# A fold product split in two, and the front's order written anew, in a fused linear attention and feed-forward kernel

## The chip, the cores and the metric

One core of one Trainium2 chip runs the kernel. TensorE (PE in the profile) does matrix products; VectorE (DVE), ScalarE (ACT) and GpSimd (POOL) work beside it, and SyncE (SP) issues transfers. The metric is the device time of one execution in microseconds.

## The reference

Linear attention with the map phi(x) = elu(x) + 1, over 8 batches of 8 heads with 576 positions of 64 numbers; its output, as 4608 rows of 512, goes through a multiplicative feed-forward.

```python
def phi(x):
    return np.where(x > 0, x, np.exp(x) - 1.0) + 1.0
q_p, k_p = (phi(q), phi(k))
kv = np.einsum('bhsd,bhse->bhde', k_p, v)
z = np.sum(k_p, axis=2)
num = np.einsum('bhsd,bhde->bhse', q_p, kv)
den = np.einsum('bhsd,bhd->bhs', q_p, z)[..., None] + 1e-06
...
a = x @ w1
b = x @ w2
h = a * b @ w3
return (h @ w_out).astype(np.float32)
```

x is num / den with the heads side by side. w1 and w2 are 512 x 1024, w3 is 1024 x 1024, w_out is 1024 x 512; all arrays are float32.

## The kernel before

The kernel multiplies w3 by w_out first (the fold) and keeps the result, wf, in bf16; so a row needs x w1, x w2, their product and one product with wf. The 4608 rows are 36 tiles of 128, and four tiles are a chunk: chunks 0 to 8. There is no scheduler: the string ORDER lists some 780 short steps, and each engine runs its share of them in that order. Waits between engines are derived from the tiles that steps read and write; a tile whose pool has no free buffer waits for the release of an older one. So a step's place fixes three things: what it stands behind on its engine, which buffer its tile gets, and whose release it waits for.

The steps that matter here (x is a batch or chunk, and so on):

- le0 to le7 (line 191) load eighths of w3, lo0 to lo3 (181) quarters of w_out, each 128 x 1024, with a cast to bf16, from POOL's queue. lw (171) loads blocks of w1 and w2. lk, lq, lv (165) load k, q, v of a batch, whole or as halves, from POOL with a + at the end and else from SP. POOL's transfers share eight semaphores in turn, so the ninth waits until the first has landed.
- H (152) are matmuls on zeros that keep TensorE running. wt (202) transposes an eighth of w3, wc (206) copies it out of PSUM, wm i.k0.k1 (212) multiplies the pieces k0 to k1 of eighth i with w_out; eight pieces are one product of the fold, and lo0 holds pieces 0 and 1, lo1 2 and 3, lo2 4 and 5, lo3 6 and 7. wd (216) copies the product to wf.
- xk, xq (226, exp on ScalarE), yk, yq (230) and zk, zq (237, both VectorE) make phi of half a batch.
- Batches 0 and 1 take another way than the rest: Z (349) sums k, K (261) makes kv, qa (330) transposes q on TensorE and qb (336) copies it, kz (361) copies kv and z, e (372) makes numerators and denominators, er (387, 388) and em (392) divide; rm (405) and rd (412, 413 on ScalarE, 415 on VectorE) do the same for the rest rows. From batch 2 on T (274) and D (320) transpose by DMA from SP, A (286) makes the product and G (304 to 308) divides.
- g c.f.w.h (428) is a first product of chunk c: w is 0 for w1 and 1 for w2; h is 0 or 1 for a half of two matmuls, 2 for all four. fc (439) copies the w1 side out, fm (448, or 446 in chunk 8) multiplies the two. O (456) is the product with wf, eight matmuls; oc (460) copies it into an o_sb tile, on VectorE with a + and else on ScalarE; S (468) stores it with two DMAs; Q8.3 (479 to 481) is the last tile.

Pools that matter: mm_ps has four banks of PSUM for wf, a, b and o products; at_ps has two buffers of two banks for the attention; o_sb has six buffers, which the a_sb of five f of chunk 0 share (line 436). A PSUM bank is freed by the copy that reads it.

At the top of ORDER all eight eighths of the fold are done as two steps of four matmuls, for example wm1.0.4 and wm1.4.8. Stores go from POOL, and for chunk 8 from SP (line 467).

Of the kernel before, what the change touches and what calls it, by code (L numbers as in the profile page):

```python
# [34 lines left out]
g1.6.1.0 rd1 g1.0.0.0 fm1.4 lq3.2 g1.3.1.1 g1.0.0.1 xk2.0 fm1.3 lv3.2 g1.6.1.1 g1.6.0.0 zk2.1 fc1.0 g1.6.0.1
g1.0.1.0 zk2.0 fc1.6 lk4.2 g1.5.0.0 fm1.6 K2.0 K2.1 g1.0.1.1 kc2.1 kc2.0+ g1.5.1.0 fm1.0 A2.0 A2.1 g1.2.1.0
G2.0 g1.2.0.0 g1.5.0.1 g1.5.1.1 fc1.5 g1.2.1.1 g1.2.0.1 fm1.5 D2.0 A2.3 fc1.2 A2.2 O0.2 yq3.1 xq3.1 fm1.2
xk3.0 G2.1 O0.1 O1.1 oc0.1 yk3.0 D2.1 xk3.1 zq3.1 O1.2 lq4.2 xk4.1 oc1.1+ zk3.0 xq3.0 A2.4 yq3.0 g2.4.0.2
yk3.1 lv5.2 g2.5.0.2 fc2.4 zq3.0 g2.5.1.2 fc2.5 G2.2 T3.1 oc1.2 g2.7.0.2 oc0.2 yk4.1 g2.4.1.2 fc2.7 vc3.0+
T3.0 g2.7.1.2 xq4.0 fm2.5 g2.2.0.2 vc3.1 zk3.1 g2.1.1.2 fm2.7 fc2.2 lv4.2 K3.0 K3.1 g2.1.0.2 kc3.1+ lk5.2  # L40
fm2.4 g2.0.0.2 fc2.1 S0.2 kc3.0 fm2.1 g2.3.0.2 xq4.1 yk4.0 g2.6.0.2 S1.1 zk4.1 fc2.0 g2.2.1.2 fc2.6 yq4.0
A3.0 xk4.0 g2.6.1.2 fm2.2 A3.1 O1.0 G3.0 g2.3.1.2 oc1.0 zk4.0 fc2.3 g2.0.1.2 S1.0 fm2.6 A3.3 A3.2 S0.0 O1.3
fm2.3 fm2.0 S0.1 G3.1 O2.2 oc1.3 D3.0 O2.1 oc2.2 vc5.0+ D3.1 vc4.1 yq4.1 lq5.2 O2.0 oc2.1 zq4.0 S2.2 vc4.0
# [2 lines left out]
g3.1.1.2 xq5.0 zq5.1 D2.2 g3.5.1.2 fm3.1 S1.2 K4.0 K4.1 fm3.5 fc3.2 g3.0.1.2 kc4.0 kc4.1+ fc3.3 zq5.0 A4.1
A4.0 g3.2.1.2 G4.0 T5.0 g3.0.0.2 g3.3.1.2 fm3.2 K5.0 D4.0 K5.1 fm3.3 fc3.0 g3.6.1.2 S1.3 kc5.0 fm3.0 A4.2
g3.7.1.2 kc5.1+ S2.1 A4.3 fm3.7 g3.6.0.2 T5.1 G4.1 fc3.6 g4.2.0.2 g4.2.1.2 fc4.2 lv6.2 g4.5.0.2 fm4.2 lq6.2
g4.3.0.2 fm3.6 fc4.5 g4.0.0.2 fc4.3 lk6.2 O3.1 fc4.0 A5.0 oc3.1+ O3.0 A5.1 oc3.0 g4.1.0.2 G5.0 S3.1 g4.5.1.2
vc6.0 D4.1 g4.0.1.2 fm4.5 g4.3.1.2 fm4.0 fc4.1 D5.0 g4.6.0.2 xq6.1 fm4.3 A4.4 g4.6.1.2 G4.2 fc4.6 g4.7.1.2  # L50
xq6.0 yq6.0 O3.3 lq7.2 yq6.1 xk6.0 fm4.6 g4.1.1.2 lk7.2 xk6.1 oc3.3+ A5.4 O3.2 fm4.1 S3.3 G5.2 D4.2 g4.7.0.2
oc3.2 zq6.0 g5.7.0.2 vc6.1+ fc4.7 g5.4.0.2 yk6.1 fc5.7 A5.2 D5.2 fm4.7 fc5.4 g4.4.0.2 zq6.1 g4.4.1.2 fc4.4
zk6.1 T6.1 xq7.0 g5.3.0.2 fm4.4 g5.3.1.2 xq7.1 yq7.0 O4.2 T6.0 yq7.1 fc5.3 zq7.0 xk7.1 O4.3 fm5.3 S3.2 oc4.2
yk7.1 xk7.0 S4.2 zq7.1 g5.7.1.2 zk7.1 oc4.3 g5.2.0.2 S4.3 fm5.7 g5.2.1.2 fc5.2 yk7.0 g5.6.0.2 S3.0 fm5.2
# [21 lines left out]
def kernel(  # L76
# [385 lines left out]
    def o_store(c, m):  # L462
        kind, b, t = order[c * (NCH // P) + m]
        for g in range(2):
            bb, j = (b, 2 * t + g) if kind == "J" else (b + g, NJ - 1)
# [2 lines left out]
            queue.dma_start(out=out[bb * S:(bb + 1) * S, :].rearrange("(p j) n -> p j n", j=NJ)[:, j, :],  # L468
                            in_=o_sbs[c, m][part])

# [128 lines left out]
```

## Time and profile before

| what | us |
|---|---|
| three runs | 246.41, 244.14, 246.7; median 246.41 |
| the profiled execution's own time | 244.84 |
| its span, first to last instruction | 243.1 |
| TensorE busy | 232.2 |
| VectorE, ScalarE, GpSimd busy | 148.9, 118.4, 60.2 |
| first fold matmul starts | 13.76 |
| first matmul of a first product starts | 33.49 |
| last matmul ends, by the chain of waits | 239.31 |

Times inside the profile count from the span's start. A row of the timeline has a start, a length, the engine (SPq for SyncE's queue), the line, the operation, what it writes and reads, how many instructions are merged, and in brackets the idle time ahead of it on that engine with what ended it. A row of a tile's view has shortest, median and longest duration in ns and the first and the last start; the line on landing gives the time from issue to landing for the instructions in that view.

### The profile page before, as it was taken

The numbers are of one execution on the slowest core, as the hardware profiler recorded it, in microseconds if no ns is written. First come the engines' busy times: TensorE is split into PE (matmuls) and PEld (weight loads), VectorE is DVE, ScalarE is ACT, GpSimd is POOL, SyncE is SP. The second block draws the span as 40 slices with busy tenths as digits, with TensorE's granted clock in tenths as the row PEclk, the third lists the DMA queues.
The fourth block names the chain that finished last, engine by engine and source line by source line (L and its number), as shares of the span: only waits on it lengthen the run. The fifth ranks groups of instructions, "written<-read, shape, count | busy, mean of one in ns | idle before, by whom it ended". The sixth has DMA issues, their size and how long they took to land.

```text
span 243.1 us, 4808 instructions
## 1 busy us (share of the span) xinstructions
PE 232.2 (96%) x1938; PEld 112.1 (46%) x1955; DVE 148.9 (61%) x280; ACT 118.4 (49%) x177; POOL 60.2 (25%) x104
## 2 busy tenths in 40 slices
...
PEclk9999999999999999999999999999999999999999
DMA  6999999998899999998699999795540002321125
GB/s 151 194 283 325 213 255 296 294 387 299 186 395 200 370 263 332 205 272 275 105 256 381 216 373 152 293 122 151 155 119 1 0 3 86 97 86 46 43 79 137
DMA packets 48470, 49.20 MB, mean 202 GB/s; under 512 B 30528, under 2 KB 34880, under 8 KB 48448
## 3 DMA queue, kind: packets, MB, share of 16 engines
...
q14 instruction: 7, 0.06, 0.1%
...
## 4 chain that ended last, share of the span: by engine, by line
PE 89%; DMA 4%; DVE 2%; ACT 1%; POOL 1%; issue 1%; POOLq 0%
PE b_ps L428 25%; PE o_ps L456 25%; PE a_ps L428 24%; PE wf_ps L212 6%; DMA wo<-in_moe_w_out_dram 4%; PE nd L286 3%; PE kvp L261 2%; POOL w3b L191 1%; PE w3p L202 1%; PE o_ps L479 1%; PE nd L372 1%; PE tq L330 1%; PE zp L349 1%; DVE k L237 1%; DVE ab L448 1%
## 5 line engine op out<-in xcount | busy, mean ns | idle before, releaser
L428 PEld LDWEIGHTS <-w_sb 128*128 128x128 bf16 x576 | 54.9, 98 | 63.9 <-issue 1.4
L468 POOL DMA_DIRECT2D out_dram<-o_sb x64 | 36.3, 571 | 157.1 <-ACT o_sb L460 72.8
L428 PE MATMUL b_ps<-xt,w_sb 128*128 128x512 bf16 x288 | 70.7, 379 | 0.0
L428 PE MATMUL a_ps<-xt,w_sb 128*128 128x512 bf16 x288 | 69.5, 379 | 0.4 <-DVE xt L392 0.3
L439 ACT COPY a_sb<-a_ps 128x512 f32<-128x512 f32 x72 | 41.7, 585 | 57.6 <-PE a_ps L428 41.6
L456 PE MATMUL o_ps<-wf_sb,ab 128*128 128x512 bf16 x266 | 63.2, 379 | 0.8 <-issue 0.2
L448 DVE TENSOR_TENSOR ab<-a_sb,b_ps 128x512 bf16<-128x512 f32 x64 | 45.8, 730 | 27.7 <-PE b_ps L428 17.8
L456 PEld LDWEIGHTS <-ab 128*128 128x128 bf16 x280 | 26.7, 98 | 31.0 <-issue 0.5
L460 ACT COPY o_sb<-o_ps 128x512 f32<-128x512 f32 x23 | 13.3, 585 | 38.4 <-PE o_ps L456 31.5
L226 ACT ACTIVATE e<-k 128x1152 bf16<-128x1152 f32 x16 | 18.3, 1161 | 12.3 <-DMA k<-in_k_dram 12.3
L226 ACT ACTIVATE e<-q 128x1152 bf16<-128x1152 f32 x16 | 18.4, 1163 | 2.4 <-DMA q<-in_q_dram 2.4
L212 PE MATMUL wf_ps<-wo,w3t 128*128 128x512 bf16 x61 | 14.7, 379 | 1.6 <-DMA wo<-in_moe_w_out_dram 1.3
L230 DVE TENSOR_SCALAR r<-k 128x1152 bf16<-128x1152 f32 x16 | 11.9, 749 | 6.1 <-DMA k<-in_k_dram 6.1
L308 DVE TENSOR_TENSOR xn<-nd,r 128x512 bf16<-128x512 f32 x24 | 15.4, 683 | 0.0
L230 DVE TENSOR_SCALAR r<-q 128x1152 bf16<-128x1152 f32 x16 | 12.5, 804 | 3.3 <-DMA q<-in_q_dram 3.3
L446 DVE TENSOR_TENSOR ab<-a_sb,b_ps 128x512 bf16<-128x512 f32 x8 | 5.5, 686 | 14.1 <-PE b_ps L428 9.4
L460 DVE COPY o_sb<-o_ps 128x512 f32<-128x512 f32 x12 | 8.3, 690 | 9.3 <-PE o_ps L456 9.0
L237 DVE TENSOR_TENSOR k<-e,r 128x1152 bf16<-128x1152 bf16 x16 | 11.8, 752 | 0.6 <-ACT e L226 0.5
L237 DVE TENSOR_TENSOR q<-e,r 128x1152 bf16<-128x1152 bf16 x16 | 11.8, 749 | 0.3
L286 PEld LDWEIGHTS <-qt 128*128 128x128 bf16 (+1 forms) x120 | 8.6, 100 | 7.2 <-issue 2.7
L286 PE MATMUL nd<-kvb,qt 128*128 128x130 bf16 (+1 forms) x120 | 11.2, 222 | 0.0
L212 PEld LDWEIGHTS <-w3t 128*128 128x128 bf16 x64 | 5.8, 98 | 8.2 <-DVE w3t L206 1.3
...
## 6 DMA issues: line engine op xcount, KB each, us to landing
...
q<-in_q_dram POOLq DMA_DIRECT2D x3, 576.0 KB, 10.4
...
```

The lines of the kernel that those rows point to most:

```text
L212: nc.tensor.matmul(wfs[i], w3ts[i][:, kc, :], wos[0][:, kc, :], start=(kc == 0), stop=(kc == FC - 1))
L226: nc.scalar.activation(out=es[name, b, c], in_=raw[name, b][:, 2 * c:2 * c + 2, :], func=AF.Exp)
L230: nc.vector.tensor_scalar(out=rs[name, b, c], in0=raw[name, b][:, 2 * c:2 * c + 2, :], scalar1=0.0, scalar2=1.0, op0=ALU.max, op1=ALU.add)
L237: nc.vector.tensor_tensor(out=ph[name, b][:, c].rearrange("p j a d -> p a j d"), in0=es[name, b, c].rearrange("p a (j d) -> p a j d", j=NJ ...
L286: nc.tensor.matmul(nd[0:n, u, 2 * c * (D + 1):2 * (c + 1) * (D + 1)], w, kvb[b % 2][:, u, c].rearrange("p a e -> p (a e)"), start=True, st ...
L308: nc.vector.tensor_tensor(out=dst.rearrange("p (i u) e -> p u i e", u=2), in0=v4[:, :, :, 0:D], in1=r[0:n].unsqueeze(3).to_broadcast([n, 2 ...
L428: nc.tensor.matmul(fps[c, f, w], (w1_sb, w2_sb)[w][:, kc, f * P:(f + 1) * P], xt[:, 4 * c:4 * c + 4, kc, :], start=(first and n == 0), sto ...
L439: nc.scalar.copy(out=fsb[c, f], in_=fps[c, f, 0])
L448: nc.vector.tensor_tensor(out=abs_[c][:, f].rearrange("p (m t g) -> p m g t", g=2, t=R), in0=fsb[c, f].rearrange("p (m g t) -> p m g t", g ...
L456: nc.tensor.matmul(o_pss[c, m], abs_[c][:, f, m * P:(m + 1) * P], wf_sb[:, f, :], start=(f == 0), stop=(f == FC - 1))
L460: copy_of(alt)(out=o_sbs[c, m], in_=o_pss[c, m])
L468: queue.dma_start(out=out[bb * S:(bb + 1) * S, :].rearrange("(p j) n -> p j n", j=NJ)[:, j, :], in_=o_sbs[c, m][part])
```

## The change

The first half of each fold product, four matmuls, becomes two steps of two: wm1.0.4 is now wm1.0.2 and wm1.2.4, so its first two matmuls need only lo0. The steps up to chunk 1 stand in a new order; from g2.4.0.2 on TensorE's order is as before. The warm-up is 11 + 3 + 2 + 3 matmuls instead of 12 + 3. Some copies change between VectorE and ScalarE. Loads come in another order: lo0 third instead of sixth, both halves of v0 ahead of k1, q2 ahead of v1. On SP, T2.0 and T2.1 stand ahead of the loads of q3 and k3. On POOL the store S0.3 moves from ahead of S0.2 to between S4.2 and S4.3; the other stores keep their order. Stores of chunk 7 go from SP instead of POOL. ORDER is one line longer, so line numbers behind it are larger by one.

The diff, cut to the lines that the text speaks of:

```diff
-i2 lq0.0 H12 le3 le0 i0 le4 le1 lo1 xq0.0 yq0.0 lo0 lo2 wt3 lo3 H3 lk0.0+ wt0 le6 wc0+ lk0.1+ wc3+ wt4 zq0.0
-le2 wt1 wc4+ lq0.1+ wc1+ qa0.0 le5 wm1.0.4 wm3.0.4 lk1.1+ wm4.0.4 le7 wm3.4.8 wm4.4.8 xk0.0 yk0.0 wm0.0.4
...
-fc0.5 g0.6.0.0 lq2.2+ g0.6.0.1 fc0.1 yk1.0 g0.1.1.0 fc0.6 g0.1.1.1 lv2.2+ g0.4.0.1 xk1.0 fm0.1 g0.2.0.0
-g0.2.0.1 fc0.4 g0.7.0.0 zk1.0 lk2.2+ g0.7.0.1 xq1.0 zk1.1 g0.0.1.0 g0.3.0.0 yq1.0 g0.3.0.1 fc0.7 g0.0.1.1
-zq1.0 xq1.1 Z1.0 Z1.1 fm0.0 qa1.0 fc0.3 g0.3.1.0 qb1.0+ kz1.1.1 g0.2.1.0 kz1.1.0 g0.3.1.1 yq1.1 fc0.2 e1.0.1
...
-em1.0.0 er1.1.0 e1.1.0 oc0.3+ O0.0 em1.1.1 S0.3 xq2.0 em1.1.0 g1.1.0.0 xq2.1 lk3.2 yq2.1 g1.7.0.0 g1.4.0.0
...
-zq4.1 A3.4 yk5.0 O2.3 T4.1 xk5.1 yk5.1 xk5.0 G3.2 g3.7.0.2 oc2.0 g3.1.0.2 zk5.1 D3.2 fc3.7 g3.4.1.2 oc2.3+
-T4.0 fc3.1 zk5.0 g3.4.0.2 vc5.1+ g3.3.0.2 fc3.4 S2.0 xq5.1 fm3.4 g3.5.0.2 yq5.1 g3.2.0.2 S2.3 fc3.5 yq5.0
...
+i2 lq0.0 H11 le6 le0 lo0 i0 le3 le1 lo1 xq0.0 yq0.0 i1 le4 wt6 lo2 H3 wc6+ lo3 zq0.0 wt0 lk0.1+ H2 wc0 i3
+wm6.0.2 lk0.0+ wm0.0.2 qa0.0 le2 wt3 H3 wc3+ lq0.1+ wm3.0.2 wt1 le5 wm3.2.4 wc1+ wm6.2.4 qb0.0+ wm1.0.2
+lv0.1+ wm1.2.4 wm0.2.4 wt4 lv0.0+ le7 wm0.4.8 wm1.4.8 wc4+ wd0 yk0.1 wm6.4.8 xk0.1 wm4.0.2 yk0.0 xk0.0
+wm3.4.8 zk0.1 wm4.2.4 wd3 lk1.0+ wt2 zk0.0 wd1 lw0.2 wc2+ Z0.0 xq0.1 lw0.0 Z0.1 kz0.1.0+ wm4.4.8 lk1.1+
...
+em0.0.0 e0.1.0 er0.1.0 wm7.0.2 em0.1.1 wm7.2.4 em0.0.1 lw1.2 wm7.4.8 wd2 em0.1.0 g0.5.0.0 wd7 g0.7.0.0
+lq2.2+ yk1.0 xk1.0 g0.5.0.1 rm0 g0.7.0.1 lv1.0+ fc0.5 zk1.0 g0.0.0.0 g0.0.0.1 fc0.7 wd5+ g0.1.0.0 lv1.1+
+fc0.0 g0.3.0.0 yk1.1 xk1.1 g0.3.0.1 g0.1.0.1 lk2.2+ g0.4.0.0 fc0.3 zk1.1 g0.2.0.0 Z1.0 fc0.1 lv2.2+ Z1.1
+kz1.1.0+ xq1.0 g0.2.0.1 yq1.0 g0.3.1.0 g0.3.1.1 rd0 zq1.0 g0.4.0.1 g0.2.1.0 fm0.3 fc0.2 qa1.0 fc0.4 g0.6.0.0
...
+yk5.0 O2.3 T4.1 xk5.1 yk5.1 xk5.0 G3.2 g3.7.0.2 oc2.0 g3.1.0.2 zk5.1 D3.2 fc3.7 S2.0 g3.4.1.2 oc2.3+ T4.0
...
+fm5.3 lv7.2 oc4.2 yk7.1 xk7.0 S4.2 zq7.1 g5.7.1.2 zk7.1 oc4.3 S0.3 g5.2.0.2 fm5.7 g5.2.1.2 fc5.2 S4.3 yk7.0
...
-            queue = nc.sync if c == NT * P // NCH - 1 else nc.gpsimd
+            queue = nc.sync if c >= NT * P // NCH - 2 else nc.gpsimd
```

More of the change, by code (lines that the diff above doesn't have):

```diff
@@ L19 @@
 ORDER = """
-i2 lq0.0 H12 le3 le0 i0 le4 le1 lo1 xq0.0 yq0.0 lo0 lo2 wt3 lo3 H3 lk0.0+ wt0 le6 wc0+ lk0.1+ wc3+ wt4 zq0.0
-le2 wt1 wc4+ lq0.1+ wc1+ qa0.0 le5 wm1.0.4 wm3.0.4 lk1.1+ wm4.0.4 le7 wm3.4.8 wm4.4.8 xk0.0 yk0.0 wm0.0.4
-wm1.4.8 qb0.0 zk0.0 wt6 i1 wd1 wm0.4.8 wc6+ xk0.1 yk0.1 wm6.0.4 wd3 lv0.0+ zk0.1 wt2 Z0.0 wd0 lv0.1+ wd4+
-Z0.1 wc2 wm6.4.8 lw0.2 kz0.1.0+ kz0.1.1+ xq0.1 lw0.0 wm2.0.4 yq0.1 i3 e0.0.1 wt5 zq0.1 er0.0.1 lw1.0 wm2.4.8
-wc5+ lk1.0+ er0.0.0 yk1.1 wm5.0.4 lw0.1 wt7 lq1.0+ xk1.1 qa0.1 wc7+ lq1.1+ wm5.4.8 qb0.1+ wd2 K0.0 lw1.1 wd6
@@ L35 @@
[L35 to L43, printed above, removed]
-zq4.1 A3.4 yk5.0 O2.3 T4.1 xk5.1 yk5.1 xk5.0 G3.2 g3.7.0.2 oc2.0 g3.1.0.2 zk5.1 D3.2 fc3.7 g3.4.1.2 oc2.3+
@@ L45 @@
-T4.0 fc3.1 zk5.0 g3.4.0.2 vc5.1+ g3.3.0.2 fc3.4 S2.0 xq5.1 fm3.4 g3.5.0.2 yq5.1 g3.2.0.2 S2.3 fc3.5 yq5.0
[L46 to L54, printed above, removed]
@@ new lines @@
+lv0.1+ wm1.2.4 wm0.2.4 wt4 lv0.0+ le7 wm0.4.8 wm1.4.8 wc4+ wd0 yk0.1 wm6.4.8 xk0.1 wm4.0.2 yk0.0 xk0.0
+wm3.4.8 zk0.1 wm4.2.4 wd3 lk1.0+ wt2 zk0.0 wd1 lw0.2 wc2+ Z0.0 xq0.1 lw0.0 Z0.1 kz0.1.0+ wm4.4.8 lk1.1+
+yq0.1 wm2.0.2 lw0.1 kz0.1.1+ e0.0.1 zq0.1 wm2.2.4 er0.0.0 wt5 lw1.1 wm2.4.8 wc5+ er0.0.1 wd6+ wm5.0.2 lq1.0+
+qa0.1 wd4 K0.0 qb0.1+ lw1.0 K0.1 wm5.2.4 kz0.0.1 wt7 kz0.0.0 e0.1.1 wc7+ e0.0.0 lq1.1+ er0.1.1 wm5.4.8
+em0.0.0 e0.1.0 er0.1.0 wm7.0.2 em0.1.1 wm7.2.4 em0.0.1 lw1.2 wm7.4.8 wd2 em0.1.0 g0.5.0.0 wd7 g0.7.0.0
@@ new lines @@
+lq2.2+ yk1.0 xk1.0 g0.5.0.1 rm0 g0.7.0.1 lv1.0+ fc0.5 zk1.0 g0.0.0.0 g0.0.0.1 fc0.7 wd5+ g0.1.0.0 lv1.1+
+fc0.0 g0.3.0.0 yk1.1 xk1.1 g0.3.0.1 g0.1.0.1 lk2.2+ g0.4.0.0 fc0.3 zk1.1 g0.2.0.0 Z1.0 fc0.1 lv2.2+ Z1.1
+kz1.1.0+ xq1.0 g0.2.0.1 yq1.0 g0.3.1.0 g0.3.1.1 rd0 zq1.0 g0.4.0.1 g0.2.1.0 fm0.3 fc0.2 qa1.0 fc0.4 g0.6.0.0
+qb1.0+ g0.1.1.0 xq1.1 g0.1.1.1 yq1.1 e1.0.1 g0.2.1.1 kz1.1.1 zq1.1 er1.0.1 g0.6.0.1 fm0.1 g0.5.1.0 g0.5.1.1
+fm0.2 er1.0.0 g0.4.1.0 g0.4.1.1 fm0.5 qa1.1 fc0.6 g0.7.1.0 fm0.4 g0.7.1.1 qb1.1 yq2.1 g0.6.1.0 g0.0.1.0
@@ new lines @@
+fm0.7 xq2.1 g0.6.1.1 g0.0.1.1 fm0.6 e1.1.1 xq2.0 K1.0 fm0.0 zq2.1 K1.1 er1.1.0 O0.3 yq2.0 kz1.0.0 zq2.0
+kz1.0.1 e1.0.0 er1.1.1 T2.0 e1.1.0 em1.0.1 O0.0 em1.0.0 oc0.3 em1.1.0 xk2.0 T2.1 g1.1.0.0 em1.1.1 g1.1.1.0
+g1.4.0.0 oc0.0 yk2.1 g1.4.0.1 xk2.1 g1.1.0.1 lq3.2 g1.1.1.1 g1.7.0.0 lk3.2 fc1.1 zk2.1 g1.7.0.1 g1.6.0.0
+fm1.1 fc1.7 g1.6.0.1 fc1.4 yk2.0 g1.3.1.0 lv3.2 g1.6.1.0 fc1.6 vc2.1+ g1.4.1.0 g1.6.1.1 vc2.0+ g1.3.1.1
+g1.4.1.1 zk2.0 g1.3.0.0 g1.3.0.1 fm1.6 rm1 K2.0 fm1.4 K2.1 g1.2.0.0 kc2.1 kc2.0+ lk4.2 g1.2.0.1 fc1.3
@@ new lines @@
+g1.7.1.0 rd1 fm1.3 g1.7.1.1 g1.5.1.0 fm1.7 fc1.2 g1.0.1.0 A2.1 A2.0 g1.2.1.0 G2.0 g1.0.0.0 g1.2.1.1 g1.0.0.1
+g1.0.1.1 fc1.0 g1.5.1.1 fm1.2 D2.0 A2.2 A2.3 g1.5.0.0 G2.1 g1.5.0.1 O0.2 fc1.5 xq3.1 fm1.5 D2.1 O0.1 xq3.0
+fm1.0 lq4.2 yq3.1 xk3.1 O1.1 zq3.1 xk3.0 yk3.0 A2.4 O1.2 oc1.1+ zk3.0 yq3.0 g2.4.0.2 oc1.2 yk3.1 lv5.2 oc0.1
+g2.5.0.2 fc2.4 zq3.0 g2.5.1.2 fc2.5 G2.2 T3.1 g2.7.0.2 oc0.2 S0.2 g2.4.1.2 yk4.1 fc2.7 xq4.0 g2.7.1.2 vc3.0+
+T3.0 S1.1 fm2.5 g2.2.0.2 vc3.1 zk3.1 g2.1.1.2 lv4.2 fc2.2 fm2.7 K3.0 xk4.1 K3.1 g2.1.0.2 kc3.1+ fm2.4 lk5.2
@@ new lines @@
+g2.0.0.2 fc2.1 kc3.0 fm2.1 g2.3.0.2 xq4.1 yk4.0 g2.6.0.2 zk4.1 fc2.0 g2.2.1.2 fc2.6 yq4.0 A3.0 xk4.0
+g2.6.1.2 fm2.2 A3.1 O1.0 G3.0 g2.3.1.2 oc1.0 zk4.0 D3.0 fc2.3 g2.0.1.2 S1.0 fm2.6 A3.3 A3.2 S0.0 O1.3 fm2.3
+fm2.0 S0.1 G3.1 O2.2 oc1.3 O2.1 oc2.2 vc5.0+ D3.1 vc4.1 S2.2 yq4.1 lq5.2 O2.0 oc2.1 zq4.0 vc4.0 zq4.1 A3.4
+yk5.0 O2.3 T4.1 xk5.1 yk5.1 xk5.0 G3.2 g3.7.0.2 oc2.0 g3.1.0.2 zk5.1 D3.2 fc3.7 S2.0 g3.4.1.2 oc2.3+ T4.0
+fc3.1 zk5.0 g3.4.0.2 S2.3 vc5.1+ g3.3.0.2 fc3.4 S1.2 D2.2 xq5.1 fm3.4 g3.5.0.2 yq5.1 S1.3 g3.2.0.2 fc3.5
```

40 lines of the change are left out of this document (21 added, 19 removed).

## The prediction, as put on record before the run

> **What bounds the kernel now.** I read the page first (shares, clock, the chain of waits), then TensorE's timeline for the places where it is not fed, then the queues and engines that decide those places.
>
> ```profile
> span 243.1 us, 4808 instructions
> PE 232.2 (96%) x1938; PEld 112.1 (46%) x1955; DVE 148.9 (61%) x280; ACT 118.4 (49%) x177; POOL 60.2 (25%) x104
> PEclk9999999999999999999999999999999999999999
> DMA  6999999998899999998699999795540002321125
> PE 89%; DMA 4%; DVE 2%; ACT 1%; POOL 1%; issue 1%; POOLq 0%
> ```
>
> TensorE is busy for 96% at the full clock, and it is 89% of the chain that ended last; the DMA engines are full until about 170 us. So a microsecond counts only if TensorE stands still in it. Its timeline, with the idle time ahead of a row in brackets (rows without a bracket follow without a gap):
>
> ```profile
> 7.24 0.62 PE L202 MATMUL w3p<-ident,w3b 128*128 128x128 bf16 x8 [1.08 <-DMA w3b<-in_moe_w_dram]
> 7.70 0.81 PE L152 MATMUL warm<-zero 128*128 128x512 bf16 x3
> 13.76 6.20 PE L212 MATMUL wf_ps<-wo,w3t 128*128 128x512 bf16 x27 [1.33 <-DMA wo<-in_moe_w_out_dram]
> 23.54 1.67 PE L212 MATMUL wf_ps<-wo,w3t 128*128 128x512 bf16 x7 [0.16 <-issue]
> 30.56 0.48 PE L261 MATMUL kvp<-v,k 64*64 64x64 bf16 x36 [0.19 <-DVE kvz L361]
> 35.71 2.32 PE L428 MATMUL a_ps<-xt,w_sb 128*128 128x512 bf16 x10 [0.32 <-DVE xt L392]
> 43.42 0.68 PE L330 MATMUL tq<-ident,q 128*128 128x128 bf16 x9
> 51.31 0.41 PE L372 MATMUL nd<-qt,kvz 64*64 64x512 bf16 x4 [0.16 <-ACT kvz L361]
> 107.52 1.03 PE L428 MATMUL b_ps<-xt,w_sb 128*128 128x512 bf16 x4
> 108.38 3.62 PE L428 MATMUL a_ps<-xt,w_sb 128*128 128x512 bf16 x16
> 168.18 1.67 PE L456 MATMUL o_ps<-wf_sb,ab 128*128 128x512 bf16 x7 [0.16 <-issue]
> ```
>
> The reader is to see that until 13.76 TensorE waits for weights, and that from there on it hardly stops: gaps of 0.16, 0.19 and 0.32 up to 35.71, one of 0.16 at 51.31, and next to nothing later. A matmul of 512 columns costs 0.216 us from start to start (107.52 to 108.38 is four), so a pair, which is one step g or one half of a split fold step, is 0.43. There is little to win: the change can pull work ahead of 13.76, and it loses each new gap in full.
>
> **The front: the split.** POOL keeps eight transfers in flight, so its next issue shows when an older one landed:
>
> ```profile
> 7.48 0.72 POOL L165 DMA_DIRECT2D k<-in_k_dram  x1 [1.08 <-DMA w3b<-in_moe_w_dram]
> 16.55 0.56 POOL L191 DMA_DIRECT2D w3b<-in_moe_w_dram  x1 [0.52 <-DMA wo<-in_moe_w_out_dram]
> 22.35 1.42 POOL L165 DMA_DIRECT2D v<-in_v_dram  x2 [5.25 <-ACT wf_sb L216]
> 25.62 1.02 POOL L147 MEMSET kvb<- 128x520 bf16 x2
> ```
>
> The first row waits for transfer 1, the second for transfer 8: (16.55 - 7.48)/7 = 1.30 us for each 256 KB, in the order of issue. Now lo0 is third instead of sixth and lands near 7.2 + 2 x 1.3 = 9.8; the new pairs wm6.0.2, wm0.0.2 and wm3.0.2 can run ahead of 13.76. That is 3 x 0.43 = 1.3 us of work moved into idle time. The four more warm-up matmuls (0.27 each by the row at 7.70) lie in gaps ahead of lo0 and of the copy of the third transposed chunk, where TensorE waited for transfers before, and cost nothing; without that cover they would cost 1.1. The earlier memset of kvb (1.02) lies in POOL's waits for landings, 1.08 and 0.52 in these rows; uncovered it would delay one load's issue, not its turn among eight in flight. Against it, lo3 is now ninth and lands near 7.2 + 8 x 1.3 = 17.6, while TensorE, from lo1 at 13.7 on, is through with six pairs and a transposed chunk (0.45) by 16.7: 0.9 of waiting. Z0.0 now needs the half of k that is eleventh (17.6 + 2 x 1.4 = 20.4, and 2.3 on ScalarE and VectorE, 22.7), TensorE is there near 22.1: 0.6. The blocks of w1 come in another order; I allow 0.3. Together 1.8 us.
>
> **The front: a new pin.** In the new order rd0 stands on ScalarE behind xq1.0, and on VectorE zq1.0 stands behind rd0, and TensorE's qa1.0 needs zq1.0. Before, rd0 was long done, and qa1.0 is the row at 43.42. The durations, and the landing of the q half:
>
> ```profile
> L165 POOL DMA_DIRECT2D q<-in_q_dram x1: 739/739/739, 29.3 to 29.3; - x1
> DMA to landing us min/median/max: 10.4/10.4/10.4
> 33.61 0.48 ACT L412 ACTIVATE rc<-ndr,eps 128x256 f32<-128x256 f32 x1
> 34.12 0.42 ACT L413 ACTIVATE rc<-rc 128x256 f32<-128x256 f32 x1
> 34.57 0.49 DVE L415 TENSOR_TENSOR xt<-ndr,rc 128x128 bf16<-128x128 f32 x2 [0.20 <-ACT rc L413]
> 40.08 1.17 ACT L226 ACTIVATE e<-q 128x1152 bf16<-128x1152 f32 x1
> 41.95 0.76 DVE L237 TENSOR_TENSOR q<-e,r 128x1152 bf16<-128x1152 bf16 x1
> ```
>
> It landed at 29.3 + 10.4 = 39.7. The loads ahead of it are as many bytes after as before (lw1.1 has changed places with lw1.0), so 39.7 is the upper end; the lower is 39.1, since POOL no longer stands without an issue for 5.25 us ahead of 22.35. I take the middle, 39.4. From there 1.2 (xq1.0) + 0.5 + 0.45 (L412, L413) + 0.45 (L415) + 0.8 (zq1.0) = 3.4: qa1.0 starts at 42.8. What TensorE has to do before it: 43.42 less its gaps (0.67), less the 1.3 pulled ahead, less three pairs of g that now stand behind qa1.0 (20 pairs before it in the old order, 17 in the new; 1.3) is 40.15, and with the 1.8 of waits 42.0. So TensorE is there 0.8 early and waits: all that the split won goes into this wait, and the waits above cost nothing more. Behind qa1.0 the three pairs still have to be done. Before, 43.42 to 51.31 is 7.89 up to e1.0.0, with 0.16 of gap; after, 7.89 - 0.16 + 1.3 = 9.03, which ends at 51.8. The front ends 0.5 us later than before (0.2 to 0.8 by the bounds of the landing). If the pin isn't there, it ends at 42.0 + 9.03 = 51.0, 0.3 earlier than before, or 0.7 if the waits are smaller.
>
> **The middle: S0.3 and its buffer.** The steps of TensorE from g2.4.0.2 on are the same, but one store has moved: S0.3, both its DMAs, from ahead of S0.2 to behind S4.2 on POOL. The next stores move up by two issues; S4.3 and the few behind it go down by two (about 1.1 us on a queue that idles there). What counts is its tile: it holds one of six o_sb buffers some 100 us longer. So each later copy into o_sb takes the buffer of a younger store. In the built program oc2.3 on VectorE waited for S0.1 and now waits for S2.2, and behind oc2.3 stands g3.4.0.2, which takes its PSUM bank. The other copies shift as well (oc2.2 to S1.0, oc2.1 to S0.0, oc2.0 to S0.1), but those stores land in time: about 3 us after issues from 95.6 on. S2.2 does not:
>
> ```profile
> L468 POOL DMA_DIRECT2D out_dram<-o_sb x1: 534/534/534, 95.6 to 95.6; - x1
> DMA to landing us min/median/max: 2.8/2.8/2.8
> L468 POOL DMA_DIRECT2D out_dram<-o_sb x2: 678/841/1004, 101.2 to 102.2; - x2
> DMA to landing us min/median/max: 8.0/8.4/8.7
> 100.35 0.59 ACT L460 COPY o_sb<-o_ps 128x512 f32<-128x512 f32 x1 [1.14 <-PE o_ps L456]
> 100.71 0.54 SPq L165 DMA_DIRECT2D q<-in_q_dram  x1
> 101.53 2.19 SPq L274 DMA_TRANSPOSE qt<-q  x1
> 105.99 0.69 DVE L460 COPY o_sb<-o_ps 128x512 f32<-128x512 f32 x1
> ```
>
> The pair of rows at 101.2 is S2.2: its second half was issued at 102.2 and landed at 110.2, because a whole head's load of q (100.71) and a transpose (101.53) share the DMA engines with it. oc2.3 ran at 105.99. Held until 110.2 plus 0.1, it ends at 111.0, and g3.4.0.2 starts there instead of at 108.38: 2.7 us of TensorE standing still, with zk5.0, vc5.1 and fm3.4 queued behind the copy on VectorE. Nothing later has slack to give it back. The bounds are 0, if S2.2 lands as the stores at 95.6 do (102.2 + 2.8 = 105.0), and 2.7. I take 2.7: the copy that starts S2.2, the load and the transpose all move with TensorE's own progress, so they meet again.
>
> The Trainium skill, "DMA: Bandwidth & Descriptors" (section "Anatomy of one DMA — SWDGE (gpsimd) path"), prices a POOL transfer at about 2.0 us plus bytes over 436 GB/s, an estimate of 2.3 us for 128 KB. By that S2.2 would be down at 104.5 and the sum would be without the 2.7. The row's 8.0 differs from it by a factor of three.
>
> **The rest.** Loads on SP and the end of the kernel:
>
> ```profile
> 45.69 0.37 SPq L165 DMA_DIRECT2D k<-in_k_dram  x1
> 232.41 0.58 ACT L460 COPY o_sb<-o_ps 128x512 f32<-128x512 f32 x1 [1.14 <-PE o_ps L456]
> 233.29 1.07 POOL L468 DMA_DIRECT2D out_dram<-o_sb  x2 [6.70 <-ACT o_sb L460]
> 234.75 4.56 SPq L468 DMA_DIRECT2D out_dram<-o_sb  x6
> ```
>
> T2.0 and T2.1 now stand ahead of q3's and k3's loads on SP, so k3 is issued after zq2.0, near 54 us, instead of at 45.69; it is used some 15 us later, and T2 itself goes out sooner than before. Without that cover k3's landing would hold the chunks behind it by up to 8 us, but its phi steps stand far behind in the order. Copies that change engines (wc0, wc2, qb0.0, oc0.3 and others) move 0.6 to 1.1 us between engines that are busy for 49% and 61%, and none of them is released late in the rows above. The stores of chunk 7 go from POOL to SP. The last of them can be issued from 233.0 to about 234.2, ahead of SP's own next at 234.75: 0 us; if it did run into them, at most 0.3, since what ends the kernel is issued behind them.
>
> **Sum.** Front +0.5, middle +2.7, the rest 0: +3.2 us on the profiled execution's 244.84, so 248.0. That execution lies 1.57 below the median of the three runs, 246.41; on the median the sum is 249.6.
>
> **Rivals.**
> 1. S2.2 lands in time, the front is pinned: +0.5, 246.9. For it: the stores at 95.6 took 2.8. Against it: the same neighbours on the DMA engines. It decides when S2.2's second half needs under 4 us.
> 2. The pin is absent (the q half lands near 38), the middle stalls: -0.7 + 2.7 = +2.0, 248.4.
> 3. The other side: the split pays and oc2.3 isn't held: -0.7, 245.7, not slower. The three pairs ahead of 13.76 are its place and 0.43 each its price; it decides when q lands before 38.5 and S2.2 before 106.
> 4. The stall is longer and TensorE's clock falls. The longest gap after work here is 1.33 at the full clock, so no row shows what 2.7 does. If the store took 1.5 longer (251.1) and the clock were halved for a few microseconds, it would be 252.5. The Trainium skill, "TensorE: Matmul & The Clock Gate" (section "What's actually happening"), puts the fall at an idle window of about 3.4 us; no run here shows it.
>
> **How the numbers follow.** The forecast (pin and stall) 0.45, rival 1 0.20, rival 2 0.15, rival 3 0.14, rival 4 0.06. The predicted time is the forecast's, 249.6; its own range is 248.8 to 250.9, from the landing of q, half a microsecond on S2.2's, and 0.5 for gaps not seen. To leave out no more than 2 in 10, the range goes from rival 3's 245.7 up to 250.9. About 1% (2.46 us) is what a measurement of this kernel can tell from no change. Slower by more: the forecast at nine in ten, rival 4 and a few hundredths of rival 2, 0.49. Faster by more needs 243.95, three times what the pairs give: 0.05. Within: 0.46.
>
> **What would show it.** Right: in the changed profile a gap of 2 to 3 us ahead of a first-product matmul of 16 near 110 us, released by the copy L461 on VectorE, which waits for a store; a gap of about 1 us ahead of the transposes of q near 43 us; fold matmuls from about 9.9 us on; the tail after the last matmul as long as before. Wrong: VectorE's copy follows its product without waiting, or the store of 101 us lands within 4 us; or TensorE has no gap between 36 and 52 us and reaches the products of chunk 1 earlier than now.

## The result, and the profile after

The changed kernel takes 248.5 us (median of 4 runs, 247.31 to 249.66), the kernel before 246.23 beside it: on record as a ratio of 1.0138, with a 95% interval of 1.0098 to 1.0177. (The two medians alone stand at 1.0092. Here and below the ratio on record is not their quotient.) The profiled execution took 247.98 us (span 246.2; 3.1 longer than before). Line numbers from here on are those of the changed kernel, one higher than before's, except where the kernel before is named.

From the page: span, busy shares, and the chain that ended last.

```profile
span 246.2 us, 4839 instructions
PE 235.5 (96%) x1959; PEld 112.9 (46%) x1959; DVE 149.1 (61%) x280; ACT 117.2 (48%) x177; POOL 55.7 (23%) x96
PE 73%; DMA 17%; ACT 3%; POOL 2%; issue 2%; DVE 1%; SPq 0%; DVEq 0%; ACTq 0%; POOLq 0%
```

TensorE's share is still 96%, so the average tells nothing. The chain does: DMA has gone from 4% to 17% of it, which says that transfers now set the time at more places. Most of it lies in front: three transfers on POOL's queue follow one another there, each issued when an older one has landed (a quarter of w_out from 5.83 to 16.25, a half of v from 16.53 to 27.1, a half of q from 27.66 to 39.87), and no work of TensorE is in the chain before 43.17. TensorE's own timeline shows where it waits; in brackets stands the idle time ahead of a row and what ended it:

```profile
7.49 1.03 PE L203 MATMUL w3p<-ident,w3b 128*128 128x128 bf16 x8 [1.43 <-DMA w3b<-in_moe_w_dram]
10.83 0.59 PE L213 MATMUL wf_ps<-wo,w3t 128*128 128x512 bf16 x2
...
43.17 0.68 PE L331 MATMUL tq<-ident,q 128*128 128x128 bf16 x9 [0.78 <-DVE q L238]
...
52.38 1.90 PE L457 MATMUL o_ps<-wf_sb,ab 128*128 128x512 bf16 x8
...
68.50 0.59 PE L429 MATMUL b_ps<-xt,w_sb 128*128 128x512 bf16 x2 [0.93 <-ACT a_sb L440]
...
80.68 1.89 PE L429 MATMUL a_ps<-xt,w_sb 128*128 128x512 bf16 x8
...
108.83 1.03 PE L429 MATMUL b_ps<-xt,w_sb 128*128 128x512 bf16 x4
111.70 3.62 PE L429 MATMUL a_ps<-xt,w_sb 128*128 128x512 bf16 x16 [1.84 <-DVE o_sb L461]
```

Subtracting the same places of the kernel before says how late each one is. O0.3 is 52.38 against 51.31 (the place with the same work ahead of it): 1.07 late. g2.4.0.2 is 80.68, and before

```profile
79.38 1.90 PE L428 MATMUL a_ps<-xt,w_sb 128*128 128x512 bf16 x8
```

so 1.30 late. Just ahead of the stall it is 108.83 - 107.52 = 1.31, behind it 111.70 - 108.38 = 3.32. So the front lost 1.07, the stretch from 52 to 80 another 0.23, the one to 108 nothing, and the stall 2.01. From the last tile's matmuls to the end it takes 0.2 less (the rows are below, beside the run on the stores). Sum: 3.1.

The two foreseen waits, followed back. First the half of q (its issue from POOL and its landing), then the steps on ScalarE and VectorE that make phi of it, with rd0 (L413 to L416) between:

```profile
L166 POOL DMA_DIRECT2D q<-in_q_dram x1: 714/714/714, 27.7 to 27.7; - x1
DMA to landing us min/median/max: 12.2/12.2/12.2
39.95 1.16 ACT L227 ACTIVATE e<-q 128x1152 bf16<-128x1152 f32 x1 [0.71 <-DMA q<-in_q_dram]
41.02 0.46 ACT L413 ACTIVATE rc<-ndr,eps 128x256 f32<-128x256 f32 x1
41.96 0.49 DVE L416 TENSOR_TENSOR xt<-ndr,rc 128x128 bf16<-128x128 f32 x2 [0.81 <-ACT rc L414]
42.37 0.75 DVE L238 TENSOR_TENSOR q<-e,r 128x1152 bf16<-128x1152 bf16 x1
```

Then store S2.2 (its two issues and their landings), and the copy oc2.3 that needs its buffer:

```profile
L469 POOL DMA_DIRECT2D out_dram<-o_sb x2: 678/806/934, 102.6 to 103.5; - x2
DMA to landing us min/median/max: 6.9/7.0/7.1
110.96 0.69 DVE L461 COPY o_sb<-o_ps 128x512 f32<-128x512 f32 x1 [3.72 <-DMA out_dram<-o_sb]
```

The reader is to see that in the first chain every row starts within a tenth of where the one before it ends, back to a landing at 27.7 + 12.2 = 39.9 (L414, not shown, runs from 41.51 to 41.93). In the second, S2.2's second half lands at 103.5 + 7.1 = 110.6, and the copy starts 0.3 behind that. This makes both waits causes as far as one profile can; the runs below test them. The wait at 68.50 has no such foreseen chain; a run below takes it up.

### The profile page after: what moved, and what is told of

Read it like the earlier page. It is cut to its first block, busy times and chain, and to the rows that moved or that the text cites. A ratio compares the mean times of both kernels' runs of the same rounds, so it can differ in the third digit from the quotient of the medians.

```text
span 246.2 us, 4839 instructions
## 1 busy us (share of the span) xinstructions
PE 235.5 (96%) x1959; PEld 112.9 (46%) x1959; DVE 149.1 (61%) x280; ACT 117.2 (48%) x177; POOL 55.7 (23%) x96
## 4 chain that ended last, share of the span: by engine, by line
PE 73%; DMA 17%; ACT 3%; POOL 2%; issue 2%; DVE 1%; SPq 0%; DVEq 0%; ACTq 0%; POOLq 0%
PE b_ps L429 23%; PE o_ps L457 22%; PE a_ps L429 22%; DMA q<-in_q_dram 5%; DMA v<-in_v_dram 4%; DMA wo<-in_moe_w_out_dram 4%; DMA out_dram<-o_sb 4%; PE nd L287 3%; PE kvp L262 2%; POOL w3b L192 1%; ACT e L227 1%; POOL wo L182 1%; PE tq L331 0%; ACT o_sb L461 0%; ACT a_sb L440 0%
## 5 line engine op out<-in xcount | busy, mean ns | idle before, releaser
L457 PE MATMUL o_ps<-wf_sb,ab 128*128 128x512 bf16 x280 | 64.3, 380 | 0.1
L469 POOL DMA_DIRECT2D out_dram<-o_sb x56 | 31.7, 571 | 143.9 <-ACT o_sb L461 71.5
L461 ACT COPY o_sb<-o_ps 128x512 f32<-128x512 f32 x24 | 13.9, 585 | 40.1 <-PE o_ps L457 33.3
L213 PE MATMUL wf_ps<-wo,w3t 128*128 128x512 bf16 x64 | 15.9, 381 | 0.4 <-ACT w3t L207 0.2
L461 DVE COPY o_sb<-o_ps 128x512 f32<-128x512 f32 x11 | 7.6, 691 | 12.1 <-PE o_ps L457 8.2
L231 DVE TENSOR_SCALAR r<-q 128x1152 bf16<-128x1152 f32 x16 | 11.9, 757 | 3.3 <-DMA q<-in_q_dram 3.3
L231 DVE TENSOR_SCALAR r<-k 128x1152 bf16<-128x1152 f32 x16 | 12.2, 770 | 0.4 <-DMA k<-in_k_dram 0.4
L207 DVE COPY w3t<-w3p 128x1024 bf16<-128x1024 bf16 x7 | 4.8, 692 | 11.5 <-PE w3p L203 9.3
## 6 DMA issues: line engine op xcount, KB each, us to landing
q<-in_q_dram POOLq DMA_DIRECT2D x3, 576.0 KB, 12.2
```

The source lines that it names most:

```text
L213: nc.tensor.matmul(wfs[i], w3ts[i][:, kc, :], wos[0][:, kc, :], start=(kc == 0), stop=(kc == FC - 1))
L231: nc.vector.tensor_scalar(out=rs[name, b, c], in0=raw[name, b][:, 2 * c:2 * c + 2, :], scalar1=0.0, scalar2=1.0, op0=ALU.max, op1=ALU.add)
L457: nc.tensor.matmul(o_pss[c, m], abs_[c][:, f, m * P:(m + 1) * P], wf_sb[:, f, :], start=(f == 0), stop=(f == FC - 1))
L461: copy_of(alt)(out=o_sbs[c, m], in_=o_pss[c, m])
```

## The experiments

All but the last are edits of ORDER; most take a step from one place and put it at another. The diffs show pieces of ORDER's lines, and ... stands for what is left out between them. Times stand beside runs of the kernel before on the same chip: its median is 245.22 for the first four runs (S0.3 and rd0), 245.12 for the two on the store's neighbours, the first on rd1 and the first on the split, and 245.39 for the others.

### S0.3 back, rd0 early, and both

```diff
-oc0.3 em1.1.0 xk2.0
+oc0.3 em1.1.0 S0.3 xk2.0
...
-zk7.1 oc4.3 S0.3 g5.2.0.2
+zk7.1 oc4.3 g5.2.0.2
```

> The changed kernel with one store step, S0.3, back ahead of chunk 0's other stores (behind em1.1.0); nothing else is touched. Theory (the kept o_sb buffer is what stops TensorE near 110 us): oc2.3 waits for S0.1 again, which has long landed, so g3.4.0.2 starts 0.86 us behind g3.4.1.2 instead of 2.87, and the time is 2.0 us under the changed kernel's, about 1.1 us over the kernel before. The wait of 0.8 ahead of qa1.0 near 43 us stays. Rival (the DMA engines are too full there, and some other store or load stops another copy): the idle time near 110 us stays within 0.5 us of 1.84 under another name, and the time is the changed kernel's.

Measured: 246.04 (6 runs), ratio 1.0056 (1.0034 to 1.0079), span 244.2. TensorE's timeline, and the copy on VectorE:

```profile
43.20 0.68 PE L331 MATMUL tq<-ident,q 128*128 128x128 bf16 x9 [0.79 <-DVE q L238]
...
108.81 1.03 PE L429 MATMUL b_ps<-xt,w_sb 128*128 128x512 bf16 x4
109.67 3.62 PE L429 MATMUL a_ps<-xt,w_sb 128*128 128x512 bf16 x16
```

```profile
107.28 0.69 DVE L461 COPY o_sb<-o_ps 128x512 f32<-128x512 f32 x1
```

The copy doesn't wait (no bracket), g3.4.0.2 comes 0.86 behind the row ahead of it, and the span is 2.0 shorter, as expected. The wait ahead of qa1.0 stays, at 0.79. The store's buffer is the cause of the stall; the rival falls.

```diff
-lv1.0+ fc0.5 zk1.0
+lv1.0+ fc0.5 rd0 zk1.0
...
-g0.3.1.1 rd0 zq1.0
+g0.3.1.1 zq1.0
```

> The changed kernel with rd0 moved up from behind xq1.0 to behind fc0.5; S0.3 stays late. Theory (rd0 behind xq1.0 pins qa1.0 to the landing of q): qa1.0 starts without idle time near 42.4 instead of 43.17, TensorE reaches O0.3 0.8 us earlier (51.6 instead of 52.38), the time is 0.8 us under the changed kernel's; the stall of 1.8 near 110 us stays. Rival (qa1.0 needs xq1.0 anyway, since zq1.0 takes its exponentials, so q's landing holds it with or without rd0): xq1.0 at 39.95 ends at 41.1, zq1.0 takes 0.8, so the idle time ahead of qa1.0 goes down only as far as TensorE is behind 42.0; then what the front lost (1.07 at O0.3 against the kernel before) stays at 0.3 or more.

Measured: 248.64 (4 runs), ratio 1.0147 (1.0096 to 1.0199), span 246.7. TensorE's timeline:

```profile
42.59 0.67 PE L331 MATMUL tq<-ident,q 128*128 128x128 bf16 x9
...
51.77 1.90 PE L457 MATMUL o_ps<-wf_sb,ab 128*128 128x512 bf16 x7
...
93.00 0.41 PE L287 MATMUL nd<-kvb,qt 128*128 128x130 bf16 x4 [0.73 <-DMA qt<-q]
...
112.17 3.61 PE L429 MATMUL a_ps<-xt,w_sb 128*128 128x512 bf16 x16 [2.06 <-DVE o_sb L461]
```

The pin is gone: qa1.0 follows without a gap, and O0.3 comes 0.61 earlier (0.8 was expected). The rival's sign came too, since 0.46 of the front's loss stays (51.77 against 51.31). In this profile a wait for a transposed q at 93.00 (0.73) and a longer stall (2.06) take the gain back; both wait for transfers, which don't land earlier just because TensorE is earlier. Whether the time is 0.8 shorter, as expected, four runs can't tell: the interval is 0.5% wide to either side, 1.3 us.

Both edits together:

> Both of the edits above. Theory: they add up, 2.8 us under the changed kernel, which is 0.3 over the kernel before in the profile (246.2 - 2.8 = 243.4 of span against 243.1), since the wait of 0.9 at 68.5 stays. Rival (one edit's gain is given back at the other's place): not more than 2.0 under the changed kernel.

Measured: 245.27 (10 runs), ratio 1.0005 (0.9986 to 1.0024), span 243.0. TensorE's timeline:

```profile
51.23 1.90 PE L457 MATMUL o_ps<-wf_sb,ab 128*128 128x512 bf16 x7
...
67.35 0.59 PE L429 MATMUL b_ps<-xt,w_sb 128*128 128x512 bf16 x2 [0.93 <-ACT a_sb L440]
```

O0.3 now comes 1.15 before the changed kernel's and 0.08 before the place with the same work of the kernel before (this profile's is the earliest; see the runs on the split). The span is 3.2 under the changed kernel's, where 2.8 was expected. So the two steps S0.3 and rd0 hold the whole loss, and the rest of the new order together, its wait of 0.93 near 68 among it, is worth nothing that can be measured.

### S0.3 late in the kernel before

```diff
-em1.1.1 S0.3 xq2.0
+em1.1.1 xq2.0
...
-zk7.1 oc4.3 g5.2.0.2
+zk7.1 oc4.3 S0.3 g5.2.0.2
```

> The kernel before with one edit: S0.3 moved behind oc4.3, as in the changed kernel. Theory: oc2.3 waits for S2.2, g3.4.0.2 starts 2.9 to 3.6 us behind g3.4.1.2 instead of 0.86, and the time is 2.0 to 2.7 us over the kernel before. Rival (S2.2 lands late only in the changed kernel, whose other stores stand elsewhere in the queue): S2.2 lands by 106 and nothing is lost.

Measured: 248.11 (4 runs), ratio 1.0119 (1.0080 to 1.0158). The profiled run is its lowest, 246.45; its timeline:

```profile
107.41 1.03 PE L428 MATMUL b_ps<-xt,w_sb 128*128 128x512 bf16 x4
110.01 3.61 PE L428 MATMUL a_ps<-xt,w_sb 128*128 128x512 bf16 x16 [1.57 <-DVE o_sb L460]
```

One moved store, alone, makes the old kernel slower by 1.2%: from start to start 2.60 instead of 0.86. That is a little under the 2.9 to 3.6 that were expected; S2.2's second half took 6.9 here, where it took 8.0 in the kernel before. The rival, that S2.2 is late only in the changed kernel, falls.

### Why the store lands late

Two kernels, one run each, with one of the store's neighbours moved away on SyncE's queue. The load is the whole q of batch 5 (1152 KB).

```diff
-S2.2 yq4.1 lq5.2 O2.0
+S2.2 yq4.1 O2.0
...
-zk5.1 D3.2 fc3.7
+zk5.1 D3.2 lq5.2 fc3.7
```

> The changed kernel with the whole head's load lq5.2 moved on SyncE's queue from ahead of T4.1 to behind D3.2, so that it is issued near 108 instead of 102.2. Theory (the load shares the DMA engines with store S2.2): S2.2's second half lands in 3 to 4 us instead of 7.0, near 107.5, and the stall ahead of g3.4.0.2 falls from 1.8 to under 0.5; something is lost again when xq5.1 waits for the load, near 113. Rival (it is the transpose T4.1, with its many short packets, that slows the store): S2.2 still takes 6 us or more, and the stall is as it was.

Measured: one run, 248.84. S2.2's landing (of its second half; the first half's isn't in the trace), and then the copy on VectorE:

```profile
DMA to landing us min/median/max: 3.4/3.4/3.4
```

```profile
107.69 0.69 DVE L461 COPY o_sb<-o_ps 128x512 f32<-128x512 f32 x1 [0.65 <-DMA out_dram<-o_sb]
```

TensorE's timeline, and xq5.1 on ScalarE:

```profile
109.50 3.62 PE L429 MATMUL a_ps<-xt,w_sb 128*128 128x512 bf16 x16
...
116.89 1.02 PE L429 MATMUL b_ps<-xt,w_sb 128*128 128x512 bf16 x4 [2.92 <-ACT a_sb L440]
```

```profile
115.20 1.16 ACT L227 ACTIVATE e<-q 128x1152 bf16<-128x1152 f32 x1 [4.06 <-DMA q<-in_q_dram]
```

The stall at 110 is gone, and a longer one of 2.92 stands at 116.89, since ScalarE's xq5.1 now waits for the load (4.06) and a copy of a first product stands behind it.

```diff
-O2.3 T4.1 xk5.1
+O2.3 xk5.1
...
-zk5.1 D3.2 fc3.7
+zk5.1 D3.2 T4.1 fc3.7
```

> The changed kernel with the transpose T4.1 moved behind D3.2 on SyncE's queue, and the load lq5.2 where it is. By the theory that the load slows store S2.2, it still takes 6 to 7 us and the stall stays at 1.8; by the rival that the transpose does, the store lands in 4 us or less and the stall is gone. If both fall short, the two share the cause.

Measured: one run, 247.52. S2.2's landing, then the copy on VectorE, then TensorE:

```profile
DMA to landing us min/median/max: 4.9/5.2/5.5
```

```profile
108.66 0.69 DVE L461 COPY o_sb<-o_ps 128x512 f32<-128x512 f32 x1 [1.48 <-DMA out_dram<-o_sb]
```

```profile
109.64 3.62 PE L429 MATMUL a_ps<-xt,w_sb 128*128 128x512 bf16 x16
...
118.25 0.64 PE L287 MATMUL nd<-kvb,qt 128*128 128x130 bf16 x8 [1.59 <-DMA qt<-q]
```

The store's second half takes 3.4 without the load, 4.9 without the transpose, 7.1 with both, so the two share the cause. Which has the larger part isn't shown: these are single runs, and with both there the other profiles have 6.9 to 10.0. Neither alone makes a stall, since the copy has slack: in this run it starts 1.48 late and g3.4.0.2 still follows at once. Moving either one only moves the wait, to whoever needs it next.

### The wait at 68.5

```diff
-rm1 K2.0 fm1.4 K2.1
+rm1 K2.0 rd1 fm1.4 K2.1
...
-g1.7.1.0 rd1 fm1.3
+g1.7.1.0 fm1.3
```

(on top of the two edits.)

> The kernel with both edits (S0.3 back, rd0 early) and a third: rd1 moved up from behind fc1.3 to behind K2.0, ahead of the copies kc2.1 and kc2.0. Theory (the wait of 0.9 at 68.5, which was not foreseen, comes from the division rd1 standing on ScalarE between the copies fc1.3 and fc1.2): the wait goes, and the time is 0.9 us under the kernel with both edits, so about 0.8 under the kernel before (ratio 0.9965). Rival (kc2.1, which waits for K2, is the late one, and fc1.3 and fc1.2 are late with or without rd1): the wait stays within 0.3 of 0.9.

Measured: 245.31 (12 runs), ratio 1.0010 (0.9994 to 1.0025). TensorE's timeline:

```profile
66.11 1.90 PE L429 MATMUL b_ps<-xt,w_sb 128*128 128x512 bf16 x8 [0.60 <-DVE ab L449]
```

The ratio of 0.9965 that was expected didn't come. ScalarE no longer holds TensorE, but VectorE does: rd1's products wait for ScalarE's part, and fm1.4 is queued behind them. So rd1 went one step further back:

```diff
-K2.0 rd1 fm1.4 K2.1
+K2.0 fm1.4 rd1 K2.1
```

> S0.3 back and rd0 early, and rd1 now behind fm1.4 instead of ahead of it (the run before showed fm1.4 queued on VectorE behind rd1's products, and TensorE waiting 0.60 for it). Theory: rd1 between fm1.4 and the copies kc2 is in nobody's way, no gap of over 0.2 is left between 60 and 120 us, and the span is 0.6 to 0.9 under that of the kernel with two edits, if TensorE reaches O0.3 at the same time. Rival (one chain of ScalarE and VectorE steps is too long here wherever rd1 stands): a gap of 0.5 or more stays near 66 to 68 us.

Measured: 244.59 (12 runs), ratio 0.9972 (0.9954 to 0.9990): a little faster than the kernel before. The profiled run is the slowest of the twelve, 245.99. TensorE's timeline:

```profile
65.46 1.89 PE L429 MATMUL b_ps<-xt,w_sb 128*128 128x512 bf16 x8
...
92.79 0.41 PE L287 MATMUL nd<-kvb,qt 128*128 128x130 bf16 x4 [1.64 <-DMA qt<-q]
```

No gap is left near 66 to 68. The one at 92.79 waits for a transpose by DMA, as the run with rd0 early did at 93.00; whether the faster runs have it isn't shown. So the expectation held at its place and not as a whole, in this run. From O0.3 to g2.4.0.2 TensorE now takes 27.21, where the changed kernel takes 28.30 and the kernel before, for the same work, 28.07: this stretch, and not the split, is where the new order gains.

### What the split is worth

On the kernel with three edits (rd1 ahead of fm1.4), the first halves in one step again:

```diff
-wm6.0.2 lk0.0+ wm0.0.2 qa0.0
+lk0.0+ qa0.0
...
-wm3.2.4 wc1+ wm6.2.4 qb0.0+ wm1.0.2
+wm3.0.4 wc1+ wm6.0.4 qb0.0+
```

(and the same for the others.)

> The kernel with all three edits, but the first half of each fold product in one step again, at the place of its second pair. So what the split itself is worth is measured where no pin can hide it. Theory (three pairs, 0.43 each, run ahead of the second load of w_out, and some of that is lost again in waits for lo3): the time is 0.3 to 1.3 us over the three edits' kernel, all of it lost before 20 us. Rival (what bounds the front from 20 us on are the loads of w1, k and q, in their order of landing, and not the fold): the place where chunk 0's output products begin (O0.3, 51.2) doesn't move by more than 0.2.

Measured: 245.14 (12 runs), ratio 0.9994 (0.9978 to 1.0010), where the split kernel had 1.0010. Z0.0 (the sums of k) and O0.3 in the two timelines, merged and split:

```profile
22.51 0.78 PE L350 MATMUL zp<-ones,k 64*64 64x64 bf16 x72 [0.40 <-DVE k L238]
...
52.30 1.90 PE L457 MATMUL o_ps<-wf_sb,ab 128*128 128x512 bf16 x7
```

```profile
22.70 0.78 PE L350 MATMUL zp<-ones,k 64*64 64x64 bf16 x72 [0.38 <-DVE k L238]
...
51.61 1.90 PE L457 MATMUL o_ps<-wf_sb,ab 128*128 128x512 bf16 x7
```

Over twelve runs each, the times don't differ by anything measurable, so the 0.3 to 1.3 that were expected didn't come. In the two profiles the split is 0.7 ahead at O0.3, and nothing eats that later: the spans are 243.8 and 243.2. But the merged profile is one of the slower of its twelve runs and the split one of the faster. With rd0 early and the split, five kernels have the same steps up to O0.3, and their profiles have it at 51.23, 51.61, 51.73, 51.77 and 52.01; so most of the 0.7 can be scatter between runs.

The rows of Z0.0 show where a gain goes. In all these profiles TensorE stands still there, for 0.22 to 0.41, until VectorE has made phi of a half of k, whose load is the eleventh on POOL's queue. What TensorE does sooner ahead of this place it waits for here, and O0.3 follows 28.9 to 29.5 behind Z0.0's start (29.8 in the merged one).

The changed kernel with the halves merged, rd0 and S0.3 as they are there:

> The changed kernel with one edit: the first half of each fold product in one step again, at the place of its second pair. S0.3 and rd0 stand as in the changed kernel. Theory (the pin at qa1.0 hides whatever the split wins): qa1.0 starts at 43.2 and O0.3 at 52.4 as in the changed kernel, within 0.2, with an idle time ahead of qa1.0 that is shorter by 0 to 0.8. Rival (the split carries the front): both come 0.4 to 1.3 later.

Measured: one run, 253.25. TensorE's timeline:

```profile
43.16 0.68 PE L331 MATMUL tq<-ident,q 128*128 128x128 bf16 x9 [0.20 <-ACT a_sb L440]
...
52.35 1.90 PE L457 MATMUL o_ps<-wf_sb,ab 128*128 128x512 bf16 x7
...
114.51 6.09 PE L429 MATMUL a_ps<-xt,w_sb 128*128 128x512 bf16 x16 [4.73 <-DVE o_sb L461]
```

qa1.0 and O0.3 stand where they stood (43.17 and 52.38), with an idle time of 0.20 instead of 0.78. That is what was expected if the pin swallows what the split wins, but this run doesn't show it cleanly: the half of q landed at 39.5, earlier than before, and xq1.0 stood behind ScalarE's own copies until 39.92, so it wasn't the landing that held it. The rest was not seen in the four runs of the changed kernel: S2.2 took longer still, and behind a stall of 4.73 the clock fell. S2.2's landing, and the stretch from 113 to 120 (busy times, then the granted clock ahead of the last two columns):

```profile
DMA to landing us min/median/max: 9.1/9.6/10.0
```

```profile
113.00:120.00 7.00, 5.49 (x14) 1.91 (x14) 4.80 (x7) 1.87 (x3) 4.97 (x8) 0.53 0.69 207
```

Sixteen matmuls took 6.09 instead of 3.62. With the 2.9 more of stall that is 5.4, and the span is 5.3 longer than the changed kernel's (251.5).

### Warm-up, and the last stores

```diff
-i2 lq0.0 H11 le6
+i2 lq0.0 H15 le6
```

(on the fastest kernel.)

> The same kernel with fifteen warm-up matmuls at the start instead of eleven (H15), which keep TensorE at work 0.9 us longer before the first block of w3. Theory (the first block's landing varies between about 6 and 8 us from run to run, and where TensorE has stood still for 1.9 us or more ahead of it, the granted clock is near 0.5 from 8 to 12 us): no window up to 12 us has a granted clock under 0.9, and the runs' mean clock is 0.997 or more in all but one or two. As for the time: where nothing pins the front, 0 to 0.5 less in the median. Rival: the clock's fall has nothing to do with that idle time, and as many runs have 0.993 or less as with eleven (7 of 12 in the kernel with three edits).

Measured: 244.88 (12 runs), ratio 0.9981 (0.9965 to 0.9997). The runs' mean clock is 0.998 or more in all twelve; with eleven warm-up matmuls it was 0.993 in six of twelve. So more work ahead of the idle time, and less idle time, do keep the clock up, and yet no time is won (244.59 with eleven). Nor are the six runs at 0.993 slower than the other six of their kernel: their medians are 244.6 and 245.0. The profile with fifteen shows why: up to 21.7 its chain of waits holds transfers (the first block of w3, then the half of k) and no work of TensorE, and Z0.0 waits 0.41 for that k.

Last, chunk 7's stores back on POOL's queue (eleven warm-up matmuls again):

```diff
-            queue = nc.sync if c >= NT * P // NCH - 2 else nc.gpsimd
+            queue = nc.sync if c >= NT * P // NCH - 1 else nc.gpsimd
```

> The kernel with rd1 behind fm1.4, and chunk 7's stores on POOL's queue as in the kernel before. Theory (the last stores' queue costs nothing): from the last matmul's start to the end of the span it takes within 0.3 of the kernel it is made from. Rival: POOL's longer issue (1.07 for two) holds its last stores and the end comes 0.5 or more later.

Measured: one run, 244.63. The last tile's first matmuls, in the kernel before, in the changed kernel and in this one:

```profile
237.39 1.91 PE L479 MATMUL o_ps<-wf_sb,ab 128*128 128x320 bf16 x16
```

```profile
240.72 1.91 PE L480 MATMUL o_ps<-wf_sb,ab 128*128 128x320 bf16 x16
```

```profile
237.20 1.91 PE L480 MATMUL o_ps<-wf_sb,ab 128*128 128x320 bf16 x16
```

To the end of the span it is 243.1 - 237.39 = 5.7, 246.2 - 240.72 = 5.5, and 242.9 - 237.20 = 5.7. In the kernel it is made from it is 5.5 too (238.73 to 244.2). In these profiles the queue is worth 0.2.

## Why the prediction was right, point by point

- **The pin.** Right in place and size of the wait: 0.8 was said, 0.78 came, and the runs with rd0 early remove it. The term of the sum was too small, 1.07 for 0.5. The half of q landed at 39.9, above the upper bound of 39.7: it was issued 1.6 earlier, but took 12.2 instead of 10.4. The step that failed was the bound "as many bytes ahead of it": the turn in the queue fixed the landing no better than within half a microsecond (39.5 to 39.9 in the five profiles with rd0 in this place). The steps behind the landing took 3.3, for 3.4, and the work behind qa1.0 52.38 - 43.17 = 9.21, for 9.03.
- **The split and the waits for loads.** TensorE was at qa1.0 at 43.17 - 0.78 = 42.39, where 42.0 was said. The profiled run had its first fold matmul at 10.83, not 9.9: the first transposes took 1.03 and not 0.62, and the warm-up and transposes behind them ran as slowly. Without the pin 51.0 was said for O0.3, 0.3 earlier than before; the five profiles with rd0 early have 51.23 to 52.01, against 51.31. So the split doesn't pay in the front even there. The wait at Z0.0 was foreseen, at 0.6; what the sum missed is that TensorE waits there with the split or without it (0.38 and 0.40 in the two profiles shown), so that the 1.3 us pulled ahead doesn't come out behind it.
- **The stall.** Right in mechanism, from the buffer to the store to the copy to the bank; undone, it goes, and put alone into the old kernel, it comes. Only the size was off: S2.2's second half took 7.1 and not 8.0, and the copy started 0.3 behind its landing and not 0.1, so 2.01 and not 2.7. The runs with its neighbours moved bear out the reason given for its lateness. The one without the load also meets rival 1's condition, under 4 us, and has no stall there. By the fit of the Trainium skill, "DMA: Bandwidth & Descriptors" (section "Anatomy of one DMA — SWDGE (gpsimd) path"), 2.3 us is an estimate for 128 KB. The nearest row, at 95.6 in the kernel before, has 2.8; this store has 3.4 without the load and 7.1 as it is, so for it the measurement decides against the estimate.
- **The rest at 0.** One wait wasn't foreseen, 0.93 at 68.50 behind rd1. The prediction took the middle from g2.4.0.2 on and said nothing of what had moved on ScalarE between O0.3 and there. The wait moved the end by less than itself (the lateness grew by 0.23 from 52 to 80), as the new order without it takes 27.21 for this stretch and the old one took 28.07. The stores' queue, put at 0, came to 0.2 the other way; the copies that changed engines weren't tried by themselves.
- **The sum.** 0.5 + 2.7 = 3.2 was said, 3.1 came: 1.07 + 0.23 + 2.01 - 0.2. Part of that is luck, since the front was put too low by 0.6 and the stall too high by 0.7. The profiled execution, 247.98, is where 248.0 was said. On the two medians the change is 2.3, by the ratio on record 3.4 (1.38% of 246.2), and 249.6 was 1.1 too high: the median of three runs that it starts from, 246.41, lies 1.0 to 1.3 over the medians of 15 to 23 runs of the same kernel that stand beside the experiments.
- **The rivals.** The gaps of 0.78 and 1.84 rule out rivals 1 to 3 for the changed kernel's profile. Rival 4 (a longer stall, and the clock falls) was seen once, in the kernel with the halves merged: 253.25, where 252.5 had been worked out for the changed kernel.
